# A long convolution whose work is ranked by a table: new ranks, a parameter batch over three blocks, and evacuations on another engine

## The chip, the core and the metric

The kernel runs on one core of one Trainium2 chip. A core has TensorE (PE: matrix products; PEld is its weight load, which overlaps it), VectorE (DVE), ScalarE (ACT), GpSimd (POOL) and SyncE (SP, which issues the DMAs here). Each engine works off its own list of instructions in order; engines wait for one another by semaphores. PE writes its results to PSUM, in "banks"; everything else lies in SBUF. The metric is the device time of one launch in microseconds. Before the change it is 681.29 us, the median of three runs (680.90 to 681.68).

## The reference, cut to what matters

For one sequence of L = 2048 tokens, D = 512 channels and N = 128 states per channel, a state space convolution is followed by a two-part mixer:

```python
A = -exp(log_A_real) + 1j * A_imag; C = (C_real + 1j * C_imag) * dt
K = 2.0 * einsum("dn,dnl->dl", C, exp(A * dt * pos)).real      # pos = 0 .. 2047
y = irfft(rfft(u, 2 * L) * rfft(K, 2 * L))[:L]                 # per channel
h = x + y + u * D_skip                                         # u = layernorm(x)
# then, on layernorm(h): tokens shifted by +-1 and +-2 between w1 and w2, gelu;
# a channel MLP, w3 - gelu - w4, with 1792 hidden channels; both added to what they read
```

The kernel's taps K, 512 channels by 2048 positions, are sums of 128 damped cosines each, and are made from tables; the convolution is done through a Fourier transform written as matrix products.

## The kernel before, in words

There are two stages. `conv_phase` makes h; `mixer_phase` does the rest and isn't touched by the change.

`conv_phase` goes over the channels in four slices s = 0 to 3 of 128, and over their tables in 32 groups g of 16 channels.

- *Parameters.* `params(t, nt)` (line 454) turns the loaded A and C of nt blocks of 128 channels into a phase, a step and an amplitude per state. It is a chain of some 35 small operations on DVE with a few on ACT (Abs, Arctan, Sin), in a buffer `scratch`. It runs for block 0, then for block 1, then for blocks 2 and 3 together. `thp` and `ini` hold steps and first phases, `ec` the amplitudes.
- *Phases and decays.* `steps(k)` (line 544) builds, on POOL, the multiples of the phases of four groups in `p8` and `s8` (`p` and `s` in the views), for eight batches. The buffers `sh` and `s` hold shifted steps that DVE writes. `decay(k)` (line 526) makes the powers `E` of the decay for two groups; its odd powers are one product on POOL.
- *Tables.* `table(g)` (line 584) adds phases on POOL (`pt<-p,s`, twice), takes Abs and two Sin on ACT (`pt<-pt`), makes the amplitudes `amx` (DVE, from `E`, with squares on ACT for the groups in `SHARE["sq"]`, one larger product otherwise) and `amy` (`amp` in the views), and multiplies both: `cs` and `sn`, three parts each. `SHARE` says for `amy`, `csy` and `sny` which groups POOL takes; the rest is DVE's.
- *Taps.* `taps(s, g)` (line 667) multiplies the tables on PE, and ACT copies the bank to `kt`.
- *The transform.* Stage A of the taps (`stage_a_taps`, `stage_a_turn`) and of x (`stage_a_x`) is PE with DVE's 32 by 32 transposes into `at`. Stage B runs in eight parts e: `product(s, e)` (line 824) multiplies on PE, ACT copies the x half of the bank to `xs`, and DVE multiplies `u<-xs,bank`. For slices 3 and 2 the x spectra are computed early by `spectrum_x` and kept in DRAM. Some parts are summed on DVE or POOL, which halves their inverse's matrix products. `stage_b_inv(s, e)` (line 880) is PE again (`bank<-u,ms`), with a copy of the bank into `at` on ACT. Then come the inverse transposes and `stage_a_inv`; for the last slice `last_a_inv`.
- *Layernorm.* `norm_x` (line 977) measures x, four of 16 rows on ACT and twelve on DVE, and normalises it, four rows on DVE and the others on ACT.

**What sets the order.** Each operation is a node of `Plan` (line 99), with an engine, a cost, the keys that it reads and writes, and a bank if it needs one. `Plan.order` (line 140) is a list scheduler: it follows the nodes in its own time and lets each engine take, among the nodes that could begin first, the most urgent. The urgency is `late`, a due time that is carried back from the nominal times in the table `NOM`. A bank is taken at the node that names it, and comes free behind the node that has `frees`. Where PE would be idle in the scheduler's time, it puts in idle products of `ident` ("fillers", function `busy`). The order of an engine's instructions is then fixed in the program, whatever the real times are. `Plan.LEAD`, `SEM` and `SAME` are the scheduler's figures for handing work over between engines.

In the views all of this has line L86, since one wrapper records every instruction; the groups are told apart by their tiles.

Of the kernel before, what the change touches and what calls it, by code (L numbers as in the profile page):

```python
# [36 lines left out]
NOM = {'lna': 5030.17, 't0': 15503.58, 'per': 1261.61, 'ln': -8507.15, 'kg0': -9569.54, 'kgs0': 3.8, 'kg': 13102.59, 'kgs': 23175.88, 'ak': 17743.24, 'ax': 8916.1, 'b': 761.28, 'ib': 10561.26, 'y': 29779.23, 'ys': 4089.19, 'tr': 15591.64, 'exp': -2330.21, 'wt': 26764.71, 'pr1': 51733.13, 'pr2': 12812.04, 'st': 40197.08, 'xa': 3425.99, 'xs': -7271.23, 'kg.1': 47920.44, 'kg.2': 14041.89, 'kg.3': -14505.47, 'kgs.1': 36068.45, 'kgs.2': 8311.11, 'kgs.3': -3109.74, 'ak.0': -2107.35, 'ak.1': 1200.57, 'ak.2': -14544.26, 'ak.3': 17291.19, 'ax.0': -10339.83, 'ax.1': 25673.75, 'ax.2': -12010.98, 'ax.3': 30089.32, 'b.0': 193.29, 'b.1': 232.39, 'b.2': 114.37, 'b.3': 29.73, 'ib.0': 8316.28, 'ib.1': -4284.85, 'ib.2': 28527.73, 'ib.3': 46308.89, 'y.0': 18162.64, 'y.1': 17123.71, 'y.2': 16697.24, 'y.3': -8517.07, 'ys.0': -6369.52, 'ys.1': 23988.28, 'ys.2': -19500.85, 'ys.3': -48947.48, 't.1': 27657.43, 't.2': -5268.68, 't.3': 14937.22}  # L37
# [61 lines left out]
class Plan:  # L99
# [9 lines left out]
    SEM = {"PE": 0.20, "ACT": 0.15, "DVE": 0.13, "POOL": 0.11, "SP": 2.4}  # L109
    SAME = {"PE": 0.0, "ACT": 0.05, "DVE": 0.05, "POOL": 0.05}  # L110
# [4 lines left out]
    def add(self, eng, cost, fn, r=(), w=(), at=None, bank=0, frees=None, dense=1.0, port=None, issue=0):  # L115
# [24 lines left out]
    def order(self):  # L140
# [32 lines left out]
        while left:  # L173
            pick = None
            for e, q in ready.items():
                cand = []
                for i in q:
# [11 lines left out]
                    cand.append((t, N[i]["late"], i))  # L189
# [124 lines left out]
def conv_phase(ctx, tc, cst, tp, h, x, log_A_real, A_imag, C_real, C_imag, log_dt, D_skip, w1, w2, fa, fi, tb, mm_):  # L314
# [20 lines left out]
    def chain(eng, cost, ops, r=(), w=()):  # L335

        for i, op in enumerate(ops):
            add(eng, cost, op, r=r, w=w, port=eng in ("DVE", "POOL"))

    NG, NS = D // CH, len(WID)  # L340
    OFF = [sum(WID[:s]) for s in range(NS + 1)]
    TS = [NOM["t0"]]
    for w_ in WID:
        TS.append(TS[-1] + NOM["per"] * w_ / 128)
    TS = [t + NOM.get(f"t.{i}", 0) for i, t in enumerate(TS)]
    nom = lambda n, s: NOM[n] + NOM[f"{n}.{s}"]
    W = max(WID)
# [7 lines left out]
    ldt, dts = cst["ldt"][:, 0:4], cst["ldt"][:, 4:8]  # L355
# [50 lines left out]
    def rates():  # L406

        rt, keys = raw[:, 0], [("raw", 0, t) for t in R4]
        add("ACT", 0.5, lambda: act.activation(rt, rt, AF.Exp), w=keys, at=-95)
# [18 lines left out]
    def transpose(t):
        al = raw[:, 1:4, t, :]
        dt = dts[:, t : t + 1]  # L430
        nom = -90 if t == 0 else NOM["tr"]
# [6 lines left out]
        p = add("PE", 0.35, tr, dense=0.0, r=[("raw", k, t) for k in range(1, 4)], bank=1, at=nom, w=[("prm", t)])  # L438
# [13 lines left out]
    scratch = tile("scratch", [128, 9, 256])  # L452

    def params(t, nt, amid=lambda: None):
# [12 lines left out]
        chain("DVE", one + 0.05, [  # L467
            lambda: v.tensor_scalar(rn, a, MAGIC, MAGIC, ALU.add, ALU.subtract),
            lambda: v.tensor_tensor(a, a, rn, ALU.subtract),
            lambda: v.tensor_scalar(rn, a, MAGIC / 32, MAGIC / 32, ALU.add, ALU.subtract),  # L470
            lambda: v.tensor_tensor(ff, a, rn, ALU.subtract),
            lambda: v.tensor_scalar(blk(stp, t, 0, nt), a, TURN, TOP, ALU.mult, ALU.min),
            lambda: v.tensor_scalar(blk(ini_, t, 0, nt), ff, -32 * TURN, TOP, ALU.mult, ALU.min),
            lambda: v.tensor_scalar(rn, ff, MAGIC / 64, MAGIC / 64, ALU.add, ALU.subtract),
            lambda: v.tensor_tensor(ff, ff, rn, ALU.subtract),
            lambda: v.tensor_scalar(blk(stp, t, 1, nt), ff, -64 * TURN, TOP, ALU.mult, ALU.min),
        ], w=kA + ks)
# [1398 lines left out]
```

## Time and profile before

| | |
|---|---|
| median of three runs | 681.29 us (680.90 to 681.68) |
| the profiled execution | 681.19 us |
| its span, first to last instruction | 679.4 us |
| granted clock of TensorE, mean | 0.986 |
| busy, whole span | PE 637.9, DVE 580.2, ACT 414.6, POOL 399.9 us |
| busy, 0 to 302 us (the convolution) | PE 265.17, DVE 274.81, ACT 239.17, POOL 226.90 us |

The profile is of one execution. Its page gives busy times of each engine over the span, then the busy share in 40 slices, the chain of work that ended last, and groups of instructions. A row of a group has the line, the engine, the operation with the tiles that it writes and reads, the shape and the count; behind the bar the busy microseconds, the mean of one in nanoseconds, and the time that the engine sat idle just before these instructions, with what ended it. A row of a table by stretches has the stretch, its length, the busy time and number of instructions of PE, PEld, DVE, ACT and POOL, then the granted clock, the share of the DMA engines and GB/s. The 1.8 us between span and time lie outside the program. `conv_phase` ends and `mixer_phase` begins near 302 us; the two overlap by a few instructions.

### The profile page before, as it was taken

The numbers are of one execution on the slowest core, as the hardware profiler recorded it, in microseconds if no ns is written. First come the engines' busy times: TensorE is split into PE (matmuls) and PEld (weight loads), VectorE is DVE, ScalarE is ACT, GpSimd is POOL, SyncE is SP. The second block draws the span as 40 slices with busy tenths as digits, with TensorE's granted clock in tenths as the row PEclk, the third lists the DMA queues.
The fourth block names the chain that finished last, engine by engine and source line by source line (L and its number), as shares of the span: only waits on it lengthen the run. The fifth ranks groups of instructions, "written<-read, shape, count | busy, mean of one in ns | idle before, by whom it ended". The sixth has DMA issues, their size and how long they took to land.

```text
span 679.4 us, 17804 instructions
## 1 busy us (share of the span) xinstructions
PE 637.9 (94%) x7224; PEld 507.9 (75%) x7224; DVE 580.2 (85%) x995; ACT 414.6 (61%) x732; POOL 399.9 (59%) x418
## 2 busy tenths in 40 slices
PE   2885999899999999999999999999999999999997
PEld 2883756673577585778888888888888889999985
DVE  6989989999998999989978799766688678988896
ACT  6998878878899886245634455545456334445430
POOL 1878489778999998402586209455511634466340
PEclk9986999999999999999999999999999999999999
DMA  8840445011201033020261523454664355434104
GB/s 216 248 161 17 149 147 148 2 49 34 65 18 34 25 100 101 17 65 1 63 194 47 178 77 140 172 171 137 210 226 133 100 170 173 138 110 140 32 0 125
DMA packets 51958, 73.58 MB, mean 108 GB/s; under 512 B 7332, under 2 KB 26788, under 8 KB 51876
## 3 DMA queue, kind: packets, MB, share of 16 engines
q1 hardware_dynamic: 50212, 69.82, 33.4%
q10 hardware_dynamic: 1152, 1.57, 0.9%
q0 software_dynamic: 512, 1.05, 0.6%
q8 instruction: 57, 0.93, 0.6%
q14 instruction: 25, 0.20, 0.1%
HBM read 44.90 MB, written 21.23 MB: 97 GB/s over the span
## 4 chain that ended last, share of the span: by engine, by line
PE 64%; ACT 9%; DVE 7%; POOL 5%; issue 3%; DMA 1%; POOLq 0%; ACTq 0%; DVEq 0%
PE l L86 20%; PE bank L86 9%; PE acc L86 7%; ACT pt L86 5%; PE l3a L86 3%; PE l3d L86 3%; PE l3b L86 3%; PE l3e L86 3%; PE l3c L86 3%; PE l3g L86 3%; PE l3f L86 3%; PE res L86 2%; DVE cs L86 2%; POOL pt L86 2%; DVE sn L86 1%
## 5 line engine op out<-in xcount | busy, mean ns | idle before, releaser
L86 POOL TENSOR_TENSOR pt<-p,s 128x512 int32<-128x512 int32 x64 | 73.4, 1161 | 8.6 <-DVE sn L86 8.1
L86 ACT ACTIVATE pt<-pt 128x1056 f32<-128x1056 int32 x64 | 69.8, 1091 | 12.4 <-DVE cs L86 6.4
L86 PE MATMUL bank<-at,tbs 128*64 128x128 f32 (+1 forms) x768 | 63.1, 311 | 2.8 <-ACT u L86 0.9
L86 PEld LDWEIGHTS bank<-at,tbs 128*64 128x64 f32 x768 | 44.7, 134 | 19.1 <-ACT at L86 2.1
L86 PE MATMUL bank<-u,ms 64*128 64x128 f32 x736 | 47.5, 278 | 5.7 <-DVE u L86 1.9
L86 PEld LDWEIGHTS bank<-u,ms 64*128 64x128 f32 x736 | 43.1, 188 | 9.7 <-DVE u L86 2.6
L86 DVE TENSOR_TENSOR cs<-pt,amx 128x512 f32<-128x512 f32 x64 | 41.2, 679 | 2.3 <-ACT amx L86 1.7
L86 PE MATMUL bank<-cs 128*32 128x64 f32 x1024 | 33.1, 228 | 10.0 <-ACT kt L86 4.0
L86 PEld LDWEIGHTS bank<-cs 128*32 128x32 f32 x1024 | 24.3, 113 | 23.8 <-POOL pt L86 6.8
L86 PE MATMUL bank<-ident 128*128 128x128 f32 x292 | 40.6, 298 | 0.0
L86 PEld LDWEIGHTS bank<-ident 128*128 128x128 f32 x292 | 37.5, 208 | 2.8 <-DVE amx L86 1.1
L86 ACT COPY at<-bank 128x512 f32<-128x512 f32 x44 | 26.9, 624 | 19.4 <-PE bank L86 19.4
L86 ACT ACTIVATE pt<-pt,halfpi 128x1056 f32<-128x1056 f32 x32 | 37.8, 1182 | 0.5
L86 POOL TENSOR_TENSOR cs<-pt,amp 128x512 f32<-128x512 f32 x26 | 31.9, 1228 | 5.5 <-ACT pt L86 2.7
L86 DVE STREAM_TRANSPOSE at<-bank 128x512 f32<-128x512 f32 (+1 forms) x36 | 32.8, 957 | 2.1 <-PE bank L86 2.0
L86 POOL TENSOR_TENSOR sn<-pt,amp 128x512 f32<-128x512 f32 x24 | 29.5, 1231 | 5.6 <-issue 4.4
L86 PE MATMUL bank<-sn 128*32 128x64 f32 x1024 | 32.5, 225 | 0.0
L86 DVE TENSOR_TENSOR u<-xs,bank 128x1024 f32<-128x1024 f32 x23 | 28.0, 1218 | 3.8 <-ACT xs L86 2.5
L86 DVE TENSOR_TENSOR amx<-E,amx 128x512 f32<-128x512 f32 (+1 forms) x32 | 25.2, 787 | 5.1 <-ACT amx L86 5.0
L86 POOL TENSOR_TENSOR cs0w<-raw,cs0w 128x512 fp32r<-128x512 f32 x5 | 6.5, 1298 | 36.5 <-ACT cs0w L86 25.5
L86 POOL TENSOR_TENSOR amp<-E,ec 128x512 f32<-128x512 f32 x23 | 25.3, 1104 | 3.9 <-DVE ec L86 3.4
L86 ACT ACTIVATE xq<-xq,qo,qr 128x512 f32<-128x512 f32 x15 | 11.0, 806 | 24.6 <-DVE qo L86 24.6
(1259 smaller groups left out, 2180.7 us busy)
## 6 DMA issues: line engine op xcount, KB each, us to landing
raw<-in_B_w_dram SPq DMA_DIRECT2D x28, 256.0 KB, 2.9
xq<-xq SPq DMA_DIRECT2D x72, 64.0 KB, 2.0
h<-in_A_u_dram SPq DMA_DIRECT2D x32, 128.0 KB, 4.1
h<-in_A_u_dram SPq DMA_DIRECT2D x16, 256.0 KB, 3.8
kept<-ptw SPq DMA_DIRECT2D x8, 512.0 KB, 4.4
ms<-in_mm_dram SPq DMA_DIRECT2D x4, 768.0 KB, 10.1
ptw<-kept SPq DMA_DIRECT2D x6, 512.0 KB, 4.4
out_dram<-h SPq DMA_DIRECT2D x48, 64.0 KB, 1.7
```

Of the source, the lines that this page charges most:

```text
L86: ins = f(*args, **kw)
```

## The change

The change leaves what is computed as it is. It does the following.

1. **Ranks.** The nominal times are gone. `RANK`, a table of 1252 whole numbers, one for each node, takes the place of `late`. Nodes of all engines are placed anew. The costs of many nodes and `SEM` and `SAME` are given other figures, and the keys are finer: for example x and y phases have keys of their own, and each parameter operation names the scratch row that it reads.
2. **Banks.** Each bank is freed behind the last node that reads it. In `rates` that is now the table load behind the seven exponentials, and in `norm_x` a copy and a product behind the square root.
3. **Parameters.** Block 0 as before; blocks 1 to 3 (channels 128 to 511) in one batch of 384 columns, in plane 1 of `at`.
4. **Steps.** `p8` and `s8` hold a whole block of 128 channels. For block 0 they are built in four pieces, x phases first (x of groups 0 to 3, y of group 0, y of 1 to 3, both of 4 to 7), for the others in one.
5. **Shares.** `SHARE` is now by absolute group or by (slice, part). To DVE instead of ACT: the `kt` copy of 7 groups (`ktv`), the copy of 7 inverse parts into `at` (`ibv`), of 4 products to `xs` (`xsv`) and of 3 early spectra (`sxv`). To DVE instead of POOL: 8 of the 16 products of odd powers (`ev`). To POOL instead of DVE: `sny` of 28 groups, before 24. Squared groups: 21, before 24. `amy` and `csy` keep their numbers on POOL (23 and 26). Summed parts: 14, before 13, 4 of them on DVE (before 6), 10 on POOL (before 7); now all eight of slice 3. Normalised on DVE: 3 rows, before 4; measured on ACT: 5, before 4.
6. **Idle products.** Seven stage A steps of the taps get two idle products each ahead of their own (`pad`).
7. **Loads.** `ldt` lies in `at`; log_A_real is the first load, and the x loads go between the parameters' loads.

```diff
-NOM = {'lna': 5030.17, 't0': 15503.58, 'per': 1261.61, ...
+RANK = (
+    143, 142, 183, 178, 179, 198, 203, 195, 202, 194, 189, 200, 208, 231, 207, 233, 220, 219, 196, 199, 223, 221, 225, 227,
...
-    SEM = {"PE": 0.20, "ACT": 0.15, "DVE": 0.13, "POOL": 0.11, "SP": 2.4}
-    SAME = {"PE": 0.0, "ACT": 0.05, "DVE": 0.05, "POOL": 0.05}
+    SEM = {"PE": 0.20, "ACT": 0.15, "DVE": 0.13, "POOL": 0.10, "SP": 2.4}
+    SAME = {"PE": 0.0, "ACT": 0.145, "DVE": 0.12, "POOL": 0.12}
...
-                    cand.append((t, N[i]["late"], i))
+                    cand.append((t, RANK[i], i))
...
+SHARE = { ... 'nrmv': [0, 2, 11], 'ktv': [4, 7, 14, 18, 19, 21, 23], 'sxv': [(2, 5), (2, 6), (3, 3)],
+  'xsv': [(0, 0), (0, 2), (0, 3), (1, 3)], 'ibv': [(0, 1), (0, 3), (1, 1), (1, 6), (2, 7), (3, 2), (3, 5)],
+  'ev': [0, 2, 7, 8, 10, 11, 13, 15], 'pad': [('a', 0, 0, 0), ('a', 0, 1, 1), ... ('t', 3, 1, 0)], ... }
+PIECES = (((range(4), (0,)), (range(1), (1,)), (range(1, 4), (1,)), (range(4, 8), (0, 1))), ((range(8), (0, 1)),))
...
-                w=["ex" if i == 6 else "eb", ("exp", i)], at=-93, frees=p if i == 6 else None)
-        add("ACT", 1.45, lambda: act.activation(tiny, halfpi, AF.Sin), r=[("exp", i) for i in range(7)], w=["trig"], at=-92)
+                w=["ex" if i == 6 else "eb", ("exp", i)])
+        add("ACT", 1.45, lambda: act.activation(tiny, halfpi, AF.Sin), r=[("exp", i) for i in range(7)], w=["trig"], frees=p)
...
+    wide = at[:, 1, 0 : 9 * 384].rearrange("p (i n) -> p i n", i=9)
...
+        for gs, xs in PIECES[min(t, 1)]:
+            n = len(gs) * len(xs) * CH
+            add("POOL", 0.82 + n * 15.9e-3, lambda gs=gs, xs=xs: grow(gs, xs), ...
...
+    def evac(name, key, n, cost, dst, src, **kw):
+
+        if key in SHARE[name]:
+            add("DVE", 0.065 + n * 1.045e-3, lambda: v.tensor_copy(dst, src()), **kw)
+        else:
+            add("ACT", cost, lambda: act.copy(dst, src()), **kw)
...
+    def pads(key, cost, dense):
+
+        n = 2 if key in SHARE["pad"] else 0
+        return n, cost + 0.23 * n, (cost * dense + 0.23 * 0.93 * n) / (cost + 0.23 * n)
...
-                have.update((t,) if t < 2 else (2, 3))
-                params(t, 1 if t < 2 else 2, *([rest] if t == 0 else []))
+                have.update((t,) if t < 1 else (1, 2, 3))
+                params(t, 1 if t < 1 else 3, *([rest] if t == 0 else []))
```

The rows below show instructions in the order in which an engine has them, before (L86) and now (L140), at three places.

**POOL, from its first computation to the first tables' phases.** `p` and `s` are the buffers of phases, `pt<-p,s` the phases of a table. Before:

```order
L86 TENSOR_TENSOR E_115<-E_115 128x96x2
L86 TENSOR_TENSOR ini<-ini 128x8x16
L86 TENSOR_TENSOR ec<-ec 128x512
L86 TENSOR_TENSOR p_120<-p_120,thp 128x32
L86 TENSOR_TENSOR p_120<-p_120,sh 128x32x2
L86 TENSOR_TENSOR p_120<-p_120,sh 128x32x4
L86 TENSOR_TENSOR s_121<-s_121 128x32
L86 TENSOR_TENSOR pt<-p_120,s_121 128x16x32 x2
```

Now:

```order
L140 TENSOR_TENSOR ec<-ec 128x512
L140 TENSOR_TENSOR p_113<-ini,p_113 128x8x16
L140 TENSOR_TENSOR p_113<-p_113,thp 128x4x16
L140 TENSOR_TENSOR p_113<-p_113,sh 128x4x16x2
L140 TENSOR_TENSOR p_113<-p_113,sh 128x4x16x4
L140 TENSOR_TENSOR s_114<-s_114 128x4x16
L140 TENSOR_TENSOR p_113<-p_113,thp 128x16
L140 TENSOR_TENSOR p_113<-p_113,sh 128x16x2
L140 TENSOR_TENSOR p_113<-p_113,sh 128x16x4
L140 TENSOR_TENSOR s_114<-s_114 128x16
L140 TENSOR_TENSOR pt<-p_113,s_114 128x16x32
```

The product of `E` moved behind the first phases, and two pieces of steps, x of four groups and y of one, stand ahead of them in place of one piece of both.

**DVE, around the first product of slice 0** (the first row `u<-xs,bank`). Before:

```order
L86 TENSOR_TENSOR cs_125<-pt,amx 128x16x32 x2
L86 TENSOR_TENSOR sn_127<-pt,amx 128x16x32
L86 SCALAR_TENSOR_TENSOR sn_127<-pt,amx 128x16x32
L86 TENSOR_TENSOR scratch<-scratch 128x256
L86 TENSOR_TENSOR amx<-E_117,amx 128x512
L86 TENSOR_TENSOR scratch<-scratch 128x256
L86 TENSOR_TENSOR u_130<-xs_132,bank_95 128x1024
L86 TENSOR_TENSOR cs_126<-pt,amx 128x16x32 x2
```

Now:

```order
L140 TENSOR_TENSOR cs_124<-pt,amx 128x16x32 x2
L140 TENSOR_TENSOR sn_126<-pt,amx 128x16x32
L140 SCALAR_TENSOR_TENSOR sn_126<-pt,amx 128x16x32
L140 TENSOR_SCALAR sh<-thp 128x256
L140 COPY xs_131<-bank_94 128x512
L140 TENSOR_TENSOR u_129<-xs_131,bank_94 128x1024
L140 TENSOR_TENSOR amx<-E_119,amx 128x512
L140 TENSOR_TENSOR u_130<-xs_132,bank_95 128x1024
L140 TENSOR_TENSOR cs_125<-pt,amx 128x16x32 x2
```

The copy to `xs`, which ACT made, is now DVE's own and stands right ahead of the product; the parameter steps that stood between tables are gone from there.

**DVE behind the last table** (from its `cs` on). Before:

```order
L86 TENSOR_TENSOR cs_126<-pt,amx 128x16x32 x2
L86 STREAM_TRANSPOSE u_131<-at 128x16x2x32
L86 TENSOR_TENSOR kt<-kt,dsk 128x16
L86 STREAM_TRANSPOSE u_130<-at 128x16x2x32
L86 STREAM_TRANSPOSE u_131<-at 128x16x2x32
L86 STREAM_TRANSPOSE at<-bank_95 128x16x32 x2
L86 STREAM_TRANSPOSE at<-bank_96 128x16x32 x2
```

Now:

```order
L140 SCALAR_TENSOR_TENSOR sn_127<-pt,amx 128x16x32
L140 TENSOR_TENSOR u_129<-xs_131,bank_97 128x1024
L140 TENSOR_TENSOR sn_127<-pt,amx 128x16x32
L140 STREAM_TRANSPOSE at<-bank_95 128x16x32 x2
L140 STREAM_TRANSPOSE at<-bank_94 128x16x32 x2
L140 TENSOR_TENSOR kt<-kt,dsk 128x16
L140 TENSOR_TENSOR u_129<-u_129 128x256 x2
L140 COPY at<-bank_95 128x4x64x2
L140 STREAM_TRANSPOSE at<-bank_94 128x16x32 x2
L140 STREAM_TRANSPOSE at<-bank_95 128x16x32 x2
```

A product and a sum of slice 2, a copy out of a bank, and eight transposes in place of four now follow the last table.

More of the change, by code (lines that the diff above doesn't have):

```diff
@@ L333, in dve @@
         return 0.065 + n * (1.045e-3 if two else 0.53e-3)
-    def chain(eng, cost, ops, r=(), w=()):
-        for i, op in enumerate(ops):
-            add(eng, cost, op, r=r, w=w, port=eng in ("DVE", "POOL"))
     NG, NS = D // CH, len(WID)
     OFF = [sum(WID[:s]) for s in range(NS + 1)]
-    TS = [NOM["t0"]]
+    W = max(WID)
+    HB = []
     for w_ in WID:
[L344 to L347, printed above, removed]
+        HB.append(0 if w_ == W else (HB[-1] + w_) % W if HB and len(HB) > 0 and WID[len(HB) - 1] < W else 0)
+    eighths = lambda s: range(HB[s] // 16, (HB[s] + WID[s]) // 16)
+    quads = lambda s: range(HB[s] // 32, (HB[s] + WID[s]) // 32)
+    whole = lambda s, i: at[:, i, 32 * HB[s] : 32 * (HB[s] + WID[s])]
     at = tile("at", [128, 2, 32 * W], where=c0)
@@ L465, in params @@
         TOP = TURN / 2 - 128
[L467 to L477, printed above, removed]
+        dv = lambda cost, op, r=(), w=(): add("DVE", cost, op, r=r, w=w, port=True)
@@ L488, in params @@
-        add("DVE", 0.02 + N * 6.6e-3, lambda: v.reciprocal(mb, ma), w=k1)
-        add("DVE", two, lambda: v.tensor_tensor(mb, mn, mb, ALU.mult), w=k1, port=True)
-        add("ACT", acts, lambda: act.activation(ma, mb, AF.Arctan), r=["trig"] + k1, w=["arc"])
-        chain("DVE", one, [
-            lambda: v.tensor_scalar(lt, c, 0.0, None, ALU.is_lt),
-            lambda: v.tensor_scalar(chunked(ng), ci, 0.0, 2.0, ALU.is_lt, ALU.mult),
-        ], r=kC + kI, w=["sign"])
-        add("ACT", acts, lambda: act.activation(sg, ma, AF.Sin), r=["trig", "arc"], w=k2)
@@ L882, in stage_b_inv @@
         n = 4 * w_
-        keys = [("a0", e, q) for q in range(8)]
-        summed = any(e in c for c in SHARE[f"sum{s}"])
+        keys = [("a0", e, q) for q in eighths(s)]
+        summed = (s, e) in SHARE["sump"] or (s, e) in SHARE["sumv"]
         terms = ((0, 0), (2, 1)) if summed else ((0, 0), (1, 3), (2, 1), (2, 2))
@@ L1006, in norm_x @@
         ]
-        for i in range(3):
+        for _ in range(3):
             ops += [
@@ L1067, in low @@
                 gp.tensor_tensor(lo, raw_, hi.bitcast(F32), ALU.subtract)
-            add("ACT", 0.5, high, r=[key], w=keys, at=late + 8)
-            add("POOL", 1.23, low, r=[key], w=keys, at=late + 9)
-    def busy(view):
-        pe.matmul(view[:, 0:FILLN], ident, ident[:, 0:FILLN], start=True, stop=True)
+            add("ACT", 0.5, high, r=[key], w=keys)
+            add("POOL", 1.32, low, r=[key], w=keys)
     cst["w1"], cst["w2"] = {}, {}
```

433 lines of the change are left out of this document (236 added, 197 removed), and 52 rows, old and new, of the table RANK.

## The prediction

> **What bounds the kernel now.** I read the page first: its engine table, then the clock row of the slices.
>
> ```profile
> span 679.4 us, 17804 instructions
> PE 637.9 (94%) x7224; PEld 507.9 (75%) x7224; DVE 580.2 (85%) x995; ACT 414.6 (61%) x732; POOL 399.9 (59%) x418
> PEclk9986999999999999999999999999999999999999
> ```
>
> PE leads over the whole span, but that average mixes two stages. The diff touches only `conv_phase`, which ends near 302 us; the mixer behind it is the same code and the same order. So I asked for the busy times of the convolution alone, cut at the places where its work changes: the start, the tables of the first 128 channels, the steady part, and what stands behind the last table.
>
> ```profile
> 0.00:20.00 20.00, 7.75 (x42) 7.41 (x43) 14.09 (x50) 14.37 (x31) 4.65 (x15) 1.00 0.85 221
> 20.00:115.00 95.00, 81.00 (x1619) 60.34 (x1620) 86.79 (x152) 81.44 (x151) 74.19 (x75) 0.91 0.48 147
> 115.00:265.00 150.00, 141.02 (x3194) 99.68 (x3193) 141.93 (x206) 130.10 (x231) 134.26 (x130) 1.00 0.16 43
> 265.00:302.00 37.00, 35.40 (x540) 24.18 (x529) 32.00 (x56) 13.26 (x24) 13.80 (x13) 1.00 0.20 59
> ```
>
> The columns behind the length are PE, PEld, DVE, ACT and POOL, then the granted clock. PE's 81.00 of 95 and 141.02 of 150 hold idle products, which fill its waits:
>
> ```profile
> L86 PE MATMUL bank<-ident 128*128 128x128 f32 x292 | 40.6, 298 | 0.0
> L86 PE MATMUL bank<-u,ms 64*128 64x128 f32 x736 | 47.5, 278 | 5.7 <-DVE u L86 1.9 <-ACT u L86 1.1 <-POOL sn L86 0.7
> ```
>
> With up to 40.6 us of such fill, PE isn't what the convolution waits for before 265 us. DVE is the fullest engine there, idle for 95 - 86.79 = 8.2 us and 150 - 141.93 = 8.1 us: 16.3 together. Behind the last table it turns round. PE is busy 35.40 of 37, and the chain of waits, whose columns are start, length and what ran, ends the convolution in one unbroken PE piece:
>
> ```profile
> 277.23 23.43 PE bank L86 x343
> ```
>
> So the convolution is DVE up to about 265 us and PE behind it. What DVE waits for, over the whole convolution (total, times, longest):
>
> ```profile
> DVE amx L86 <- ACT amx L86: 5.0, 6, 2.9
> DVE at L86 <- ACT at L86: 4.7, 2, 3.0
> DVE u L86 <- ACT xs L86: 2.5, 5, 1.1
> DVE cs L86 <- ACT amx L86: 1.7, 3, 1.0
> DVE u L86 <- ACT at L86: 1.3, 3, 0.9
> ```
>
> The larger waits are for ACT: 15.2 us in these five rows. A second loss is hidden in DVE's busy time. The same size of work takes different times, in the groups by shape (count, busy us, mean ns):
>
> ```profile
> L86 DVE TENSOR_TENSOR cs<-pt,amx 128x512 f32<-128x512 f32 x64 | 41.2, 679 | 2.3 <-ACT amx L86 1.7 <-ACT pt L86 0.3
> L86 DVE TENSOR_TENSOR sn<-pt,amp 128x512 f32<-128x512 f32 x8 | 7.5, 935 | 0.6 <-ACT pt L86 0.6
> L86 DVE TENSOR_TENSOR cs<-pt,amp 128x512 f32<-128x512 f32 x6 | 7.0, 1166 | 0.0
> L86 DVE TENSOR_TENSOR amp<-E,ec 128x512 f32<-128x512 f32 x9 | 8.2, 916 | 0.0
> L86 DVE TENSOR_SCALAR h<-h,mvh,bs 128x512 f32<-128x512 f32 x4 | 3.5, 941 | 0.0
> L86 DVE TENSOR_TENSOR scratch<-scratch 128x128 f32<-128x128 f32 x10 | 4.4, 465 | 0.1
> L86 DVE TENSOR_TENSOR thp<-thp,scratch 128x128 f32<-128x128 f32 x2 | 0.6, 289 | 0.0
> L86 DVE TENSOR_TENSOR scratch<-scratch 128x256 f32<-128x256 f32 x5 | 4.0, 802 | 0.0
> L86 DVE TENSOR_TENSOR ini<-ini 128x256 f32<-128x256 f32 x2 | 0.8, 422 | 0.0
> ```
>
> Against 679 ns, the multiplications by `amp` lose 8 x 256 + 6 x 487 + 9 x 237 ns = 7.1 us; `h` against 679 loses 1.0; the two scratch shapes against 289 and 422 lose 10 x 176 + 5 x 380 ns = 3.7 us. Together 11.8 us, an estimate. They are operations that read and write SBUF while POOL works; products that read a bank don't lengthen. The Trainium skill, "SBUF — State Buffer", section "SBUF: two separate sides", says that a DVE operation with two SBUF inputs and a GpSimd operation lock a shared port for the whole instruction and the loser waits; these rows agree (935 and 1166 beside 679).
>
> So what an order can win back up to 265 us is 16.3 of idle time and 11.8 of lengthening: 28.1 us. That is the ceiling, and nothing else in the diff is large.
>
> **The change part by part.** *Evacuations to DVE.* Counting the tables of `SHARE`, 7 `at` and 7 `xs` or far copies of 128x512 go from ACT to DVE, and 7 `kt` copies of 128x256. DVE's price for such a copy out of a bank stands in the mixer, and for a small one at the start; ACT's prices:
>
> ```profile
> L86 DVE COPY xh<-l4x x2: 693/693/693, 562.9 to 563.6; 128x512 f32<-128x512 f32 x2
> L86 DVE COPY ec<-bank x1: 374/374/374, 7.7 to 7.7; 128x128 f32<-128x128 f32 x1
> L86 ACT COPY at<-bank 128x512 f32<-128x512 f32 x44 | 26.9, 624 | 19.4 <-PE bank L86 19.4
> L86 ACT COPY xs<-bank 128x512 f32<-128x512 f32 x24 | 13.8, 579 | 3.5 <-PE bank L86 3.5
> L86 ACT COPY kt<-bank 128x256 f32<-128x256 f32 x32 | 11.2, 372 | 1.6 <-PE bank L86 1.4
> ```
>
> 14 x 0.693 = 9.7 us. The 128x256 copy lies between 0.374 and 0.693; by length that is 0.48, so 7 x 0.48 = 3.4 (2.6 to 4.9). DVE gets 13.1 us; ACT loses 7 x 0.624 + 7 x 0.579 + 7 x 0.372 = 11.0.
>
> *Odd powers `E`.* Eight of 16 go from POOL to DVE. 192 elements lie between the 0.289 and the 0.802 above; I take 0.47, near the uncontended middle: 3.8 us (2.3 to 6.4). POOL loses 8 x 0.766 = 6.1 us:
>
> ```profile
> L86 POOL TENSOR_TENSOR E<-E 128x192 f32<-128x192 f32 x16 | 12.3, 766 | 19.0 <-ACT E L86 18.8
> L86 POOL TENSOR_TENSOR sn<-pt,amp 128x512 f32<-128x512 f32 x24 | 29.5, 1231 | 5.6 <-issue 4.4 <-POOL pt L86 0.5 <-ACT pt L86 0.4
> ```
>
> *Work taken from DVE.* Four `sn` products go to POOL: -4 x 0.935 = -3.7, and 4 x 1.231 = +4.9 there. Four sum operations fewer at 0.528: -2.1. Three groups fewer are squared: they take one 128x896 product instead of a 128x512 one, 3 x (1.084 - 0.688) = +1.2. One row of `h` fewer is normalised (0.94 above) and one fewer measured (0.68), and the step that took 1.07 beside POOL reads a bank instead, where its like takes 0.19: -2.5.
>
> ```profile
> L86 DVE TENSOR_TENSOR u<-u 128x256 f32<-128x256 f32 x8 | 4.0, 528 | 0.0
> L86 DVE TENSOR_TENSOR amx<-E,amx 128x896 f32<-128x896 f32 x8 | 8.7, 1084 | 3.4 <-ACT amx L86 3.4
> L86 DVE TENSOR_TENSOR amx<-E,amx 128x512 f32<-128x512 f32 x24 | 16.5, 688 | 1.7 <-ACT amx L86 1.6
> L86 DVE SCALAR_TENSOR_TENSOR bs<-mvh,bs 128x16 f32<-128x16 f32 x1 | 1.1, 1068 | 0.0
> L86 DVE SCALAR_TENSOR_TENSOR bs<-mvh,bank 128x16 f32<-128x16 f32 x3 | 0.6, 185 | 0.1
> L86 DVE BATCH_NORM_STATS2 bs<-h 128x6 f32<-128x512 f32 x12 | 7.8, 680 | 0.0
> L86 DVE RECIPROCAL scratch<-scratch 128x128 f32<-128x128 f32 x2 | 1.9, 954 | 0.1
> L86 DVE RECIPROCAL scratch<-scratch 128x256 f32<-128x256 f32 x1 | 1.8, 1753 | 0.0
> ```
>
> *Parameters in one batch.* One pass over 384 columns replaces one over 128 and one over 256. What is saved is each operation's fixed part, 2 x c(128) - c(256): 2 x 0.954 - 1.753 = 0.155 for the reciprocal, 2 x 0.465 - 0.802 = 0.13 for each of five products. At this 0.13 for the 20 other steps too, an estimate: -3.4 (-2 to -4; no row shows a pass over 384 columns).
>
> DVE's sum: 13.1 + 3.8 - 3.7 - 2.1 + 1.2 - 2.5 - 3.4 = **+6.4 us** (3.5 to 9). Of this the order puts 4 transposes `at<-bank` of 0.722 and 3 copies of 0.693 behind the last table, and 2 sums fewer: +3.9. So DVE gets +2.5 up to the last table.
>
> ```profile
> L86 DVE STREAM_TRANSPOSE at<-bank 128x512 f32<-128x512 f32 x20 | 13.3, 722 | 0.0
> ```
>
> *Behind the last table* PE had 72 inverse matmuls (`bank<-u,ms` and the same from `thp` and `ini`) by the order and now has 88, since two inverses come later. A matmul makes two records of 47.5 / 736 = 0.0645 us: 16 x 0.129 = +2.1. DVE, busy 32.00 of 37 there, gets +3.9 and stays inside. I take +2.9, between PE's price and DVE's.
>
> *Costed at nothing.* The idle products: 14 of 40.6 / 146 = 0.28 us, which stand where fills stood; without that cover they'd cost 3.9. If they lift the clock in the slice marked 6, PE isn't the bound in it. POOL: +4.9 - 6.1, six more sum operations and larger steps, about +2 on an engine idle for 21 of 95 us and 16 of 150. The start: POOL builds the first phases behind more small steps, up to 2 us late, and DVE has 5.9 idle us in its first 20; log_A_real's load goes ahead, up to 0.5 early. The late x phases are next in line there. Freeing a bank at its last reader costs no instruction.
>
> *The order.* For a gain: 15.2 us of the waits are for ACT, and ACT has 11 us less to do; and the lengthened kinds of operation become fewer (`sn` by `amp`, `h`, the parameter steps). Against it: DVE is already busy 95% of the steady part, and a gap filled early can come back late. Bounds are 0 and 28.1; I take a third, **-9.4**, nearer to nothing, since a full engine seldom gets all its waits back.
>
> Sum, on the profiled execution's 681.19 us (its span 679.4 and 1.8 around it; the median is 681.29, 0.1 more): 681.2 + 2.5 + 2.9 - 9.4 = 677.2, rounded **677**.
>
> **The rivals.**
>
> *A, slower: DVE is the wall.* Place: 115 to 265 us, DVE 141.93 of 150. Each copy that ACT gave up stands in DVE's queue before the next table's product, and the 8.1 us of idle time there are short waits for chains of ACT and POOL that any order has. If less than the 5.4 us that the sum adds return of the 28.1, the change loses; with none back it is 681.2 + 5.4 = 686.6, and 687.6 if DVE's whole 6.4 count. For it: DVE is already the fullest, 0.693 us there replaces 0.579 to 0.624 on ACT. Against: ACT, idle only 13.6 of 95 us in the first tables, is what DVE waits for. The Trainium skill, "Perfetto Trace Analysis", section "Optimizing Scalar/DVE Operations", says to move work from a saturated DVE to Scalar, and puts Scalar's fixed part on PSUM at some 51 ns against 125 for DVE; the sign agrees with these copies, and by that rule A would be the result.
>
> *B, no change.* About 5.4 us return, as much as is added: 681, give or take 1.4. For it: the two longest waits, 3.0 and 2.9 us, are single chains of ACT that another order may leave whole. Against it: nothing ties the two amounts together.
>
> *C, much faster.* Two thirds return: 681.2 + 5.4 - 18.7 = 667.9. For it: nearly every wait names ACT, and the parameter passes, which lengthen most, shrink. Against: POOL stays at 134.26 of 150 us, so most of the lock stays.
>
> *D, the order is bound by ACT's table chain,* not by DVE: then its 11.0 us less show up whole, and the tail's 2.9 come on top: 681.2 - 11.0 + 2.9 = 673. For it: the five waits above. Against it: ACT is idle 13.6 of 95 and 19.9 of 150 us.
>
> **How the numbers follow.** Forecast 0.36, D 0.12, C 0.14: faster 0.62. B 0.14. A 0.24. A difference under 0.2% (1.4 us) can't be told from no change. The likeliest case's own range is 672 to 680; for 8 in 10 the range reaches into C and A, leaving out C's far end and the worst of A: **668 to 686**.
>
> **What would show it.** Right: DVE's busy time in the convolution at most some 6 us above the 274.8 that the four rows add up to (less where the lock shrinks), idle time between 20 us and the last table down from 16.3 by half or so, `cs<-pt,amp` and `sn<-pt,amp` nearer 679, the last table done before 260 us, and PE unbroken behind it for some 2 us longer. Wrong: the same DVE idle with more busy time (A), waits of DVE for PE's banks in place of those for ACT (B), or a first product later than 115 us. The mixer should keep its 679.4 - 302 = 377 us; a change there would make the working wrong from its first step.

## The result and the profile after

The changed kernel takes 677.12 us (median of six runs, 676.15 to 678.51), against 680.94 us before (six runs, 680.04 to 681.68). The ratio is 0.9948, with a 95% interval of 0.9932 to 0.9963: 3.8 us faster. The profiled execution is the fastest of the six, 676.15 us with a span of 673.9; against the profiled execution of before that is 5.0 us.

The page of the changed kernel, its engines and the clock row:

```profile
span 673.9 us, 17729 instructions
PE 641.1 (95%) x7226; PEld 508.9 (76%) x7226; DVE 575.4 (85%) x991; ACT 403.9 (60%) x700; POOL 398.8 (59%) x411
PEclk9989999999899999999999999999999999999999
```

I cut both convolutions at two places that mean the same in each: the end of the last product `cs` or `sn` on DVE, and the start of DVE's first `xq<-h,mvh,rr` of the mixer. The columns are as before: PE, PEld, DVE, ACT, POOL, clock. Before:

```profile
0.00:264.47 264.47, 229.26 (x4822) 167.01 (x4822) 242.81 (x407) 225.55 (x410) 212.57 (x218) 0.97 0.32 94
264.47:300.50 36.03, 34.55 (x537) 23.57 (x538) 30.51 (x53) 12.31 (x21) 14.33 (x13) 1.00 0.21 60
```

After:

```profile
0.00:253.96 253.96, 227.46 (x4778) 165.10 (x4786) 233.73 (x399) 215.68 (x379) 203.84 (x202) 0.98 0.34 96
253.96:294.80 40.84, 39.18 (x586) 26.60 (x574) 35.22 (x58) 11.68 (x21) 21.68 (x21) 1.00 0.22 66
```

The last table is done 10.5 us earlier. DVE's busy time up to it falls by 9.1 us (242.81 to 233.73), and its idle time only from 21.7 to 20.2. Behind it the end takes 4.8 us longer. The convolution so ends 5.7 us earlier; the mixer takes 378.9 us before and 379.1 now.

DVE got more to do, and yet is busy for less. The groups by shape tell why. After:

```profile
L140 DVE TENSOR_TENSOR cs<-pt,amx 128x512 f32<-128x512 f32 x64 | 41.6, 679 | 2.1 <-ACT pt L140 1.5 <-ACT amx L140 0.5
L140 DVE TENSOR_TENSOR sn<-pt,amp 128x512 f32<-128x512 f32 x4 | 3.4, 844 | 0.0
L140 DVE TENSOR_TENSOR cs<-pt,amp 128x512 f32<-128x512 f32 x6 | 4.3, 715 | 0.0
L140 DVE TENSOR_TENSOR amp<-E,ec 128x512 f32<-128x512 f32 x9 | 7.0, 773 | 0.1
L140 DVE TENSOR_SCALAR h<-h,mvh,bs 128x512 f32<-128x512 f32 x3 | 1.8, 587 | 0.0
L140 DVE TENSOR_TENSOR scratch<-scratch 128x128 f32<-128x128 f32 x5 | 1.3, 270 | 1.7 <-ACT scratch L140 1.7
L140 DVE COPY at<-bank 128x512 f32<-128x512 f32 x7 | 4.8, 686 | 0.0
L140 DVE COPY kt<-bank 128x256 f32<-128x256 f32 x7 | 2.9, 417 | 0.2 <-PE bank L140 0.2
L140 DVE TENSOR_TENSOR E<-E 128x192 f32<-128x192 f32 x8 | 3.9, 486 | 0.0
L140 DVE RECIPROCAL at<-at 128x384 f32<-128x384 f32 x1 | 2.6, 2553 | 0.0
```

`cs<-pt,amp` is down from 1166 to 715 ns, `sn<-pt,amp` from 935 to 844, `amp<-E,ec` from 916 to 773, `h` from 941 to 587, and a parameter product of 128 columns from 465 to 270, while `cs<-pt,amx`, whose second input is in a bank, stays at 679. (`amx` lies in a bank, though it isn't PE that writes it.) A window of before shows one case whole. The columns are start, duration, engine and instruction; DVE:

```profile
54.92 0.68 DVE L86 TENSOR_TENSOR cs<-pt,amx 128x512 f32<-128x512 f32 x1
55.51 2.28 DVE L86 TENSOR_TENSOR scratch<-scratch 128x128 f32<-128x128 f32 x2
```

and POOL over the same time:

```profile
54.48 2.09 POOL L86 TENSOR_TENSOR pt<-p,s 128x512 int32<-128x512 int32 x2 [0.35 <-DVE sn L86]
56.53 1.12 POOL L86 TENSOR_TENSOR amp<-E,ec 128x512 f32<-128x512 f32 x1
```

Two parameter products, of a shape that takes 0.29 us elsewhere, take 2.28 together, beside POOL operations of 1.06 to 1.12 us that follow one another without a gap. Each of the two ends 0.15 us behind a POOL instruction: 56.72 behind 56.57, and 57.80 behind 57.65.

To put a number on it over all instructions up to the end of the convolution, I took for each operation and shape its duration at the 10th percentile over both traces (an overlap with the instruction before is counted once), called everything above it lengthening, and what is left work. This is worked out, not a row of a view; it is used for all runs below alike. "End" is the start of the mixer's `xq` on DVE in the profiled execution, whose own time is in the last column: a row is one execution, not the median.

| run | end | DVE work | lengthening | idle | median time | profiled execution |
|---|---|---|---|---|---|---|
| before | 300.5 | 238.8 | 34.5 | 27.2 | 680.9 | 681.2 |
| the change | 294.8 | 246.1 | 22.8 | 25.8 | 677.1 | 676.2 |
| order alone | 300.1 | 234.0 | 25.5 | 40.6 | 679.6 | 681.0 |
| copies on ACT | 296.4 | 235.9 | 25.0 | 35.5 | 676.9 | 677.8 |
| 7 `at` copies on ACT | 294.3 | 241.9 | 23.9 | 28.5 | 676.7 | 675.6 |
| E on POOL | 298.0 | 244.1 | 21.9 | 31.9 | 679.2 | 679.1 |
| before, copies on DVE | 311.6 | 248.9 | 35.0 | 27.7 | 689.9 | 692.4 |
| before, half phases | 297.2 | 238.7 | 27.7 | 30.8 | 677.6 | 678.0 |
| before, new figures | 317.4 | 238.3 | 35.3 | 43.8 | 700.4 | 700.3 |
| order blind to the port | 341.2 | 244.9 | 38.5 | 57.7 | 722.2 | 722.1 |
| no idle products | 299.7 | 246.0 | 25.6 | 28.0 | 676.9 | 680.9 |

The first two rows are the result: work +7.3, lengthening -11.7, idle -1.4, end -5.7 us. Not all that is called lengthening has to do with POOL. Of the 34.5 us of before, 23.9 lie on instructions that neither read nor write a bank and overlap one of POOL's, and of the 22.8 after, 12.8; all the rest is 10.6 and 10.0. So nearly the whole difference lies where both engines work on SBUF at once. By groups, the parameter steps went from 10.8 to 2.8 us of it, the products that make or use `amp` from 7.3 to 1.9, and `h` from 1.7 to 0.2; the others rose by 3.1 together. Some of these instructions are also fewer now: four `sn` products and one row of `h` left DVE, and the parameters take two passes in place of three.

### The profile page after: what moved, and what is told of

Its sections match the earlier page's. It is cut to its first block, busy times and chain, and to the rows that moved or that the text cites. A ratio compares the mean times of both kernels' runs of the same rounds, so it can differ in the third digit from the quotient of the medians.

```text
span 673.9 us, 17729 instructions
## 1 busy us (share of the span) xinstructions
PE 641.1 (95%) x7226; PEld 508.9 (76%) x7226; DVE 575.4 (85%) x991; ACT 403.9 (60%) x700; POOL 398.8 (59%) x411
## 4 chain that ended last, share of the span: by engine, by line
PE 70%; DVE 13%; ACT 7%; issue 3%; POOL 3%; DMA 3%; SPq 1%; DVEq 0%; ACTq 0%; POOLq 0%
PE l L140 20%; PE bank L140 14%; PE acc L140 7%; ACT pt L140 4%; DVE at L140 4%; PE l3e L140 3%; PE l3a L140 3%; PE l3d L140 3%; PE l3g L140 3%; PE l3f L140 3%; PE l3b L140 3%; PE l3c L140 3%; PE res L140 2%; DVE cs L140 2%; DMA h<-in_A_u_dram 2%
## 5 line engine op out<-in xcount | busy, mean ns | idle before, releaser
L140 POOL TENSOR_TENSOR pt<-p,s 128x512 int32<-128x512 int32 x64 | 70.9, 1120 | 6.7 <-DVE sn L140 6.0
L140 ACT ACTIVATE pt<-pt 128x1056 f32<-128x1056 int32 x64 | 69.8, 1097 | 7.6 <-DVE cs L140 4.6
L140 PE MATMUL bank<-at,tbs 128*64 128x128 f32 (+1 forms) x768 | 65.1, 314 | 2.6 <-ACT kt L140 0.9
L140 PEld LDWEIGHTS bank<-at,tbs 128*64 128x64 f32 x768 | 45.3, 135 | 18.7 <-DVE at L140 2.5
L140 PE MATMUL bank<-u,ms 64*128 64x128 f32 x736 | 47.6, 279 | 0.6 <-DVE u L140 0.4
L140 PEld LDWEIGHTS bank<-ident 128*128 128x128 f32 x310 | 37.7, 198 | 13.1 <-issue 5.2
L140 PEld LDWEIGHTS bank<-u,ms 64*128 64x128 f32 x736 | 43.0, 188 | 5.8 <-issue 2.2
L140 DVE TENSOR_TENSOR cs<-pt,amx 128x512 f32<-128x512 f32 x64 | 41.6, 679 | 2.1 <-ACT pt L140 1.5
L140 PE MATMUL bank<-ident 128*128 128x128 f32 x310 | 41.7, 288 | 0.8 <-DVE at L140 0.7
L140 POOL TENSOR_TENSOR cs<-pt,amp 128x512 f32<-128x512 f32 x26 | 32.6, 1255 | 9.4 <-ACT pt L140 5.4
L140 ACT ACTIVATE pt<-pt,halfpi 128x1056 f32<-128x1056 f32 x32 | 38.0, 1186 | 0.1
L140 POOL TENSOR_TENSOR sn<-pt,amp 128x512 f32<-128x512 f32 x28 | 34.0, 1217 | 3.8 <-issue 2.0
L140 ACT COPY at<-bank 128x512 f32<-128x512 f32 x37 | 23.1, 627 | 21.5 <-PE bank L140 21.4
L140 PE MATMUL bank<-cs 128*32 128x64 f32 x1024 | 32.4, 224 | 2.4 <-DVE cs L140 1.3
L140 DVE STREAM_TRANSPOSE at<-bank 128x512 f32<-128x512 f32 (+1 forms) x36 | 33.2, 948 | 1.1 <-PE bank L140 1.0
L140 PEld LDWEIGHTS bank<-cs 128*32 128x32 f32 x1024 | 23.8, 110 | 13.4 <-issue 4.2
L140 PE MATMUL bank<-sn 128*32 128x64 f32 x1024 | 31.9, 221 | 0.3 <-issue 0.2
L140 DVE TENSOR_TENSOR u<-xs,bank 128x1024 f32<-128x1024 f32 x23 | 27.9, 1216 | 3.4 <-ACT xs L140 3.0
L140 PE MATMUL bank<-h,fas 32*32 32x512 f32 x256 | 23.1, 752 | 6.8 <-ACT h L140 5.8
L140 DVE TENSOR_TENSOR amx<-E,amx 128x512 f32<-128x512 f32 (+1 forms) x32 | 26.4, 825 | 3.2 <-ACT amx L140 3.0
L140 POOL TENSOR_TENSOR cs0w<-raw,cs0w 128x512 fp32r<-128x512 f32 x5 | 6.5, 1299 | 36.5 <-ACT cs0w L140 36.3
L140 POOL TENSOR_TENSOR amp<-E,ec 128x512 f32<-128x512 f32 x23 | 24.6, 1074 | 4.1 <-DVE E L140 2.7
```

The costliest lines, as they stand in the source:

```text
L140: ins = f(*args, **kw)
```

## The experiments

Theory L says that the gain is the lengthening which the new order avoids, that DVE is the bound, and that the copies given to it are a cost. Theory R says that ACT's relief by these copies is the gain.

**The copies back on ACT, in the new order.** The scheduler still counts them on DVE, so that nothing else moves.

```diff
         if key in SHARE[name]:
-            add("DVE", 0.065 + n * 1.045e-3, lambda: v.tensor_copy(dst, src()), **kw)
+            add("DVE", 0.065 + n * 1.045e-3, lambda: act.copy(dst, src()), **kw)
```

> The changed kernel with its order kept word for word, but the 21 copies out of a bank that it gives to VectorE are made by ScalarE, at the same place of the program. Theory L (the gain is less lengthening of VectorE's operations by a better order; the copies are a cost): VectorE loses 7 x 0.686 + 7 x 0.68 + 7 x 0.417 = 12.5 us of work before and behind the last table, ScalarE gains 11 us, VectorE is still the bound, and the time falls to 669 to 675. Theory R (the gain is ScalarE's relief): ScalarE's chain of Abs and Sin gets the 11 us back, VectorE's waits for it grow by at least 4 us, and the time is 679 to 686.

676.93 us, ratio to before 0.9938 (0.9921 to 0.9954): the same as the change. Both theories miss. The rows of this run, busy times and then what DVE waited for between 20 and 262 us:

```profile
0.00:255.99 255.99, 226.72 (x4778) 163.96 (x4786) 227.38 (x381) 222.26 (x397) 203.46 (x202) 0.99 0.33 95
255.99:296.40 40.41, 39.10 (x588) 26.55 (x576) 33.52 (x55) 13.49 (x24) 21.64 (x21) 1.00 0.24 67
```

```profile
DVE amx L140 <- ACT amx L140: 8.6, 13, 2.0
DVE u L140 <- ACT xs L140: 3.4, 5, 1.6
```

In the changed kernel the same two waits, over the same stretch, are:

```profile
DVE u L140 <- ACT xs L140: 3.0, 3, 2.3
DVE amx L140 <- ACT amx L140: 3.0, 7, 1.0
```

DVE works 10.2 us less and sits idle 9.7 us more, above all before `amx`, which ACT starts. So the copies do relieve ACT, as R has it, and DVE pays for it in full, as L has it. In this order no gain or loss by them shows in the time.

**The seven `at` copies alone back on ACT.**

```diff
-            add("DVE", 0.065 + n * 1.045e-3, lambda: v.tensor_copy(dst, src()), **kw)
+            add("DVE", 0.065 + n * 1.045e-3, lambda: act.copy(dst, src()) if name in ("ibv",) else v.tensor_copy(dst, src()), **kw)
```

> The changed kernel with its order, of the 21 copies only the 7 of inverse parts into at back on ScalarE. If each copy is worth the same nothing on either engine, 677 within 0.2%. If the seven stand where VectorE is full (three of them behind the last table, where ScalarE is busy 12 of 41 us), 674 to 676. If ScalarE's chain is what holds the order, 678 to 680.

676.70 us, 0.9950 (0.9923 to 0.9977): no difference from the change, the first of the three cases.

**The same copies on DVE in the order of before.**

```diff
-        add("ACT", 0.27, lambda: act.copy(k, plan.view(p)...), w=[key], frees=p)
+        add("ACT", 0.27, lambda: moved("kt", g, k, plan.view(p)...), w=[key], frees=p)
...
+    def moved(n, key, d, s):
+        v.tensor_copy(d, s) if key in MOVED[n] else act.copy(d, s)
```

> The kernel before with its order, but the copies out of a bank of the same groups and parts as in the change (7 to kt, 7 to at, 4 to xs, 3 early spectra) made by VectorE at the same place of the program. Theory L: VectorE gets 12.5 to 13.1 us of work, of which its 16 us of waits hide less than half: 687 to 692. Theory R: waits for ScalarE shrink by as much as is added or more: 676 to 682.

689.85 us, 1.0140 (1.0122 to 1.0158): 9.0 us slower, as L expects. DVE's work grows by 10.1 us and its idle time hardly moves (27.2 to 27.7): nothing of ACT's 8.1 us less of busy time comes back. The order of before has no room for the copies; the new one, with the moves that come with it, has.

**Nearly the order alone:** the copies on ACT and the eight products `E` on POOL, in the new order. The parameter batch and the smaller moves of point 5 stay in.

```diff
-            add("DVE", 0.065 + n * 1.045e-3, lambda: v.tensor_copy(dst, src()), **kw)
+            add("DVE", 0.065 + n * 1.045e-3, lambda: act.copy(dst, src()), **kw)
...
-        eng = v if k in SHARE["ev"] else gp
+        eng = gp
```

> The changed kernel with its order, but the 21 copies on ScalarE and the 8 products of odd powers of the decay on GpSimd, as before the change: nearly the new order alone. Theory L: VectorE has 16.4 us less work than the changed kernel, GpSimd 6.4 us more; 669 to 677. Theory R: ScalarE and GpSimd are late for VectorE again, and the time is that of before or worse, 680 to 690.

679.58 us, 0.9983 (0.9969 to 0.9997): faster than before by a little over 1 us, and between what the two theories expected. The lengthening is 9.0 us below that of before and the work 4.8 below, but the idle time is 13.4 above. Without the engine moves the new order has less lengthening and more waiting.

**The products `E` on POOL, the copies on DVE.**

```diff
-        eng = v if k in SHARE["ev"] else gp
+        eng = gp
```

> The changed kernel with its order and its copies, but the 8 products of odd powers of the decay that it gave to VectorE on GpSimd again, at the same place. VectorE loses 8 x 0.486 = 3.9 us, GpSimd gets 8 x 0.8 = 6.4. Theory L (VectorE is the bound): 673.5 to 676. Rival (the table chain through GpSimd and ScalarE is as long as VectorE's, as the two runs with and without copies suggest): 678 to 681.

679.15 us, 0.9973 (0.9957 to 0.9989): some 2 us slower than the change, at the edge of the intervals. The rival holds: DVE works 2.0 us less and idles 6.1 more. The two runs with the copies on ACT are a second pair for the same move, 676.93 with these products on DVE and 679.58 with them on POOL, and there the intervals lie apart (0.9921 to 0.9954, 0.9969 to 0.9997). These eight small products on DVE are the one engine move that the runs show to pay.

**All sixteen `E` products on DVE,** alone, with the seven `at` copies on ACT, and with all 21 on ACT. Of the first, the edit is `eng = v` in the line above.

> The changed kernel with its order, with all 16 products of odd powers on VectorE instead of 8. Giving 8 back to GpSimd cost 2.0 us and made VectorE wait 6.1 us more. Theory C (the products stand in a chain GpSimd - ScalarE - VectorE, and VectorE's own 0.49 us is shorter than GpSimd's 0.80 and the two hand-overs): the other 8 are worth as much, 674 to 676. Rival (the 8 were those that hold the chain; VectorE gets 3.9 us more work): 677 to 681.

> As the run with all 16 products of odd powers on VectorE, and the 7 copies of inverse parts into at on ScalarE, which alone stood at 676.7. Theory C: 673 to 675.5, faster than the change. Rival (nothing adds up, since the end is set by chains that both leave whole): 676 to 678.

> As the run with all 16 products on VectorE, and all 21 copies on ScalarE. VectorE has 12.5 - 3.9 = 8.6 us less work than in the change. Theory C: 673 to 676. Theory of a flat optimum (what VectorE loses it waits for ScalarE): 676 to 679.

They take 680.75 (0.9995, 0.9984 to 1.0006), 679.26 (0.9975, 0.9967 to 0.9984) and 679.85 us (0.9984, 0.9975 to 0.9993). The chain theory fails in all three: the other eight products cost 2.6 to 3.6 us against the run with the same copies and eight, by the medians. (By the ratios it is 1.7 to 3.2, and with the seven copies on ACT the intervals overlap.) Of the three other expectations only the first holds; the other two times lie above both of their ranges. In the first, DVE's lengthening rises from 22.8 to 24.9 us, its work by 1.5 and its idle time by 1.5. No mix of these moves beats the change clearly.

**POOL's phases halved, in the order of before.** From the third group on each addition covers half its channels and leaves the other half out, so only the times are of use.

```diff
-            n = CH
+            n, m = CH, CH if g < 2 else CH // 2
...
-                pi.rearrange("p (d i) -> p d i", i=33)[:, i * n : i * n + n, 0:32]...
+                pi.rearrange("p (d i) -> p d i", i=33)[:, i * n : i * n + m, 0:32]...
```

> The kernel before with its order, but from the third group on each addition of phases on GpSimd covers half its channels (the other half keeps what stood there, so the tables are not the right ones); GpSimd loses about 60 x 0.55 = 33 us, VectorE runs the same instructions. Theory P (the lengthening of VectorE's operations on SBUF is waiting for GpSimd's instruction in progress): the lengthening falls by a quarter or more, VectorE's busy time up to the end of the convolution from 273 us to 260 to 267, and the products cs by amp from 1.17 us to under 1.0 or remain only where another GpSimd operation runs. Rival (it comes from ScalarE, the banks or the shape): VectorE's busy time stays at 271 to 275 us whatever the total time does.

677.60 us (two executions), 0.9950 (0.9930 to 0.9970). DVE runs the same instructions, and is busy for 6.9 us less than before. By window, and by group, with POOL's row of before last:

```profile
0.00:261.20 261.20, 228.20 (x4822) 166.85 (x4822) 235.92 (x407) 225.92 (x410) 185.39 (x218) 0.97 0.33 95
261.20:297.20 36.00, 34.56 (x536) 23.42 (x536) 30.49 (x53) 12.40 (x21) 14.47 (x13) 1.00 0.20 60
```

```profile
L86 DVE TENSOR_TENSOR cs<-pt,amp 128x512 f32<-128x512 f32 x6 | 5.1, 851 | 0.0
L86 POOL TENSOR_TENSOR pt<-p,s 128x256 int32<-128x256 int32 x60 | 42.3, 721 | 11.2 <-DVE sn L86 10.6
L86 POOL TENSOR_TENSOR pt<-p,s 128x512 int32<-128x512 int32 x64 | 73.4, 1161 | 8.6 <-DVE sn L86 8.1
```

`cs<-pt,amp` falls from 1166 to 851 ns though nothing of it was touched. Theory P of the expectation holds for most of what the run moved (the part on instructions that touch no bank and overlap POOL's is 16.3 us, from 23.9), and the rival, that the lengthening comes from elsewhere, falls. The lengthening, 27.7 us from 34.5, fell by a fifth and not by the quarter expected. Since 6.9 us less on DVE gave 3.6 us less time, half of it went into waits again. POOL itself has 27 us less to do here, but DVE waits more and not less, so the shorter waits of DVE for POOL's results aren't the gain. This one intervention on POOL gave nearly the time of the whole change.

**The order blind to the port.** The scheduler's rule that keeps DVE's and POOL's operations on SBUF apart is taken out; operations, engines and ranks stay. The scheduler of before has the same rule, so the rule isn't what the change brought; the run tells what it is worth in the new order.

```diff
-                    if N[i]["port"] and owner != e:
-                        t = max(t, taken - self.LEAD[e])
```

> The changed kernel with its ranks and engines, but its scheduler no longer keeps VectorE's and GpSimd's operations on SBUF apart when it orders them (the rule on the shared port is left out of the order; the operations are the same). Theory L: the lengthening comes back: the 6 products cs by amp on VectorE go from 0.72 us to 0.9 or more, VectorE's busy time up to the end of the convolution rises from 269 us by 4 to 10 us, and the time is 680 to 690. Theory R: the lengthening stays near the changed kernel's, and the time is within 676 to 680.

722.23 us, 1.0616 (1.0585 to 1.0647). The lengthening does come back, 38.5 us, and the group of L's expectation with it:

```profile
L140 DVE TENSOR_TENSOR cs<-pt,amp 128x512 f32<-128x512 f32 x6 | 6.7, 1114 | 1.3 <-ACT pt L140 1.3
```

But the time is far above both ranges. Lengthening explains 15.7 us of the 46 by which the convolution ends later; 32 are idle time. That the order was drawn up for durations that don't come true would explain these, but no run shows it.

**The new figures in the old scheduler.**

```diff
-    SEM = {"PE": 0.20, "ACT": 0.15, "DVE": 0.13, "POOL": 0.11, "SP": 2.4}
-    SAME = {"PE": 0.0, "ACT": 0.05, "DVE": 0.05, "POOL": 0.05}
+    SEM = {"PE": 0.20, "ACT": 0.15, "DVE": 0.13, "POOL": 0.10, "SP": 2.4}
+    SAME = {"PE": 0.0, "ACT": 0.145, "DVE": 0.12, "POOL": 0.12}
```

> The kernel before, engines and due times as they are, with only the change's figures for handing work over between and on the engines in the scheduler. If these figures are what keeps VectorE and GpSimd apart: VectorE's lengthening of 34.5 us falls below 30 and the time below 679. If the ranks and the early parameter batch do it: lengthening 33 to 40 us, and a time of 681 or more, since the due times were set for other figures.

700.41 us, 1.0283 (1.0267 to 1.0299), lengthening 35.3 us. The figures by themselves keep nothing apart; with the due times and costs of before they give a worse order.

**No idle products.**

```diff
-                for _ in range(n):
+                for _ in range(0):
                     busy(plan.view(ids[jp])[:, 0, :])
```

> The changed kernel with its order, without the 14 idle products ahead of seven stage A steps. My prediction: no difference, 676.5 to 678, TensorE's clock between 20 and 115 us not below 0.95. Rival (they hold the clock): the clock there falls towards the 0.91 of before, and the time is 678.5 to 682.

676.91 us in the median of ten, 0.9932 (0.9903 to 0.9961): no difference in the time, as expected. The clock missed the expectation. In the profiled execution, at 680.93 us one of the slower of the group, it is 0.93 between 20 and 115 us, not 0.95 or more:

```profile
20.00:115.00 95.00, 82.61 (x1623) 61.35 (x1623) 88.69 (x156) 81.24 (x139) 77.16 (x78) 0.93 0.51 154
```

The change has 0.96 there:

```profile
20.00:115.00 95.00, 84.95 (x1739) 63.78 (x1740) 90.64 (x162) 83.10 (x145) 79.29 (x79) 0.96 0.51 154
```

Nine of the ten executions without the products spread from 673.16 to 681.22 us; the tenth took 1253.46 and has no trace. The six of the change lie between 676.15 and 678.51. That the idle products narrow the spread is only suggested. Over the nine, time and mean granted clock go together: the three fastest, up to 673.54 us, had 0.993 to 0.995, and the two slowest, from 680.93 us, 0.985 and 0.982. Which makes the other, no run shows. The row of this run in the table above is of one of its slower executions, and has little of the change's gain left.

## Why the prediction was right, and where it was not

The time was right, 677 forecast and 677.12 measured, and so was its sign. Of its steps some held and some cancelled.

- *DVE's added work.* +6.4 forecast, +7.3 by the work column. The two aren't quite one measure, since some of what the forecast took off DVE was priced with its lengthening (`sn` at 0.935, the step of 1.07). The prices were near: 0.686 for a copy of 512 where 0.693 stood, 0.417 for 0.48, 0.486 for 0.47, and 2.553 for the reciprocal of 384 columns, 0.15 less than its two passes, as worked out.
- *Behind the last table.* +2.9 forecast, +4.8 measured. DVE's +3.9 there was +4.7. PE's price of +2.1 was too small: the inverse matmuls came to that, but stage A of the last slice slid behind the cut as well. PE's rows of the two tails, before and then after:

```profile
L86 PE MATMUL bank<-u,ms 64*128 64x128 f32 x67 | 4.8, 281 | 0.0
L86 PE MATMUL bank<-kt,fas 32*32 32x512 f32 x32 | 1.1, 600 | 0.0
```

```profile
L140 PE MATMUL bank<-u,ms 64*128 64x128 f32 x112 | 7.6, 281 | 0.0
L140 PE MATMUL bank<-kt,fas 32*32 32x512 f32 x48 | 3.3, 600 | 0.0
```

- *What the order wins back.* -9.4 forecast, out of 16.3 of idle time and 11.8 of lengthening; measured 13.1, and nearly all of it lengthening (11.7), with 1.4 of idle time. This is the step that was mis-sized, and its reason was half wrong. It put forward that the waits for ACT are 15.2 us and that ACT has 11 less to do. That was a misreading of its own rows: they are of the whole convolution, and 5.6 of the 15.2 us lie ahead of 20 us or behind the last table, outside the stretch whose 16.3 us were to be won. Between 20 us and the last table all waits for ACT were 10.8 us before and are 10.2 now. DVE's idle time up to the last table fell by 1.4 us only, and between 20 us and the last table from 15.8 to 13.4, where the prediction's own sign was half. The run with the copies on ACT shows the two sides equal. The other half, that fewer operations meet POOL's, carries the gain by the table, and the halved phases show where such lengthening comes from. The words "nearer to nothing, since a full engine seldom gets all its waits back" held for waits and not for lengthening, of which the groups named in the prediction lost most: by its own measure the `amp` products fall from 7.1 us to 4 x 0.165 + 6 x 0.036 + 9 x 0.094 = 1.7. The parameter steps were sized too small from the start: 3.7 us for two of their shapes, where all of them together hold 10.8 by the measure of the table.
- *The errors cancel.* Up to the last table 3.6 us too little gain, behind it 1.9 too little loss. The profiled execution gained 5.0 us and the medians 3.8; the sum said 4.0.
- *Rival A* named DVE as the wall and took the copies for a loss. In the old order that is right, and by 9.0 us; in the new one it isn't. The rule of the Trainium skill that the prediction cited, on the page "Perfetto Trace Analysis", section "Optimizing Scalar/DVE Operations", that taking work off a saturated DVE may make sense, holds in the first case; in the second the same copies change nothing.
- *Rival D*, the table chain through ACT as the bound, is closer than its chance of 0.12 said: with the copies on ACT, DVE is idle for nearly as long as it was relieved. That fits two chains about equally long in the new order, and would explain why none of the moves tried on the changed kernel beats it; it isn't shown by itself.
- *The start* was costed at nothing; the first product `u<-xs,bank` begins at 111.4 us instead of 115.2, so nothing was lost there. The idle products were costed at nothing, and the median agrees.

What stays open: how much of the avoided lengthening is due to the new ranks, how much to the early parameter batch, whose steps on DVE lie between 25 and 92 us instead of 55 and 160. The parameter steps hold the larger share of it, but whether for the batch or for its new place the runs didn't part, nor the finer keys, the new costs of the nodes and the freeing of the banks from the ranks. Open too is the clock: between 20 and 115 us the change has 0.96 granted where 0.91 was before, and what of the 3.8 us goes with it was not tested. The accounts of DVE's time rest on one execution of each kernel, for the change its fastest of six.

## What to carry to other kernels

A busy share can hide waiting: before counting an engine as the wall, compare the durations of one shape, and if the same operation takes 0.3 us in one place and 1.2 in another, look at what the other engine on SBUF does in that moment. Price a move between engines in the order in which it will run: the same 21 copies cost 9 us in one order and nothing in another. Where a scheduler's order was drawn up for its own assignment, an engine move at fixed order tells what that assignment is worth in that order alone, and not what a new order could make of the move.

## What the runs showed of the hardware

- DVE operations with both inputs in SBUF lengthened beside a run of POOL instructions: two products of 128x128 took 1.21 and 1.15 us instead of 0.29, and each ended 0.15 us behind a POOL instruction. DVE operations with an input in a bank stayed at 679 ns beside the same POOL work. Halving 60 POOL instructions of about 1.16 us (0.72 then) took 6.9 us off DVE's busy time without a change to DVE.
- PE's granted clock between 20 and 115 us was 0.91 before, 0.96 in the change and 0.93 without the 14 idle products, though idle products made up 38 to 42 us of the convolution in all three. Time and mean clock go together over the executions without the 14; no run here shows that the time follows from the clock.
